# A scheduler's price for changing the matmul shape: 0.1 between three kinds becomes 0.175 between two

## The chip, the core and the metric

The kernel runs on one core of one Trainium2 chip. A core has five engines, each with an instruction queue of its own that it works through in order: TensorE (PE in the profile; its weight loads are listed as PEld), VectorE (DVE), ScalarE (ACT), GpSimd (POOL) and SyncE (SP), which here issues the DMAs. Engines wait for each other through semaphores. The metric is the device time of one execution in microseconds (us), the median of several runs.

## The reference

A retention layer (attention with a causal decay instead of a softmax) for 8 batches of 8 heads, 576 positions, 64 wide, and then an MLP with a PReLU on the 4608 x 512 result. All is fp32.

```python
scores = scale * np.matmul(q, k.transpose(0, 1, 3, 2))
gamma = 1.0 - 2.0 ** (-5.0 - np.arange(H, dtype=np.float32))
rel = pos[:, None] - pos[None, :]
Dmat = np.where(rel >= 0, gamma[:, None, None] ** rel[None, :, :], 0.0)
x = np.matmul(scores * Dmat[None], v)        # then (B,H,S,D) -> (B*S, H*D)
h = x @ w_in                                 # 512 -> 2048
g = np.maximum(h, 0.0) + alpha * np.minimum(h, 0.0)
return g @ w_out                             # 2048 -> 512
```

## The kernel before

**Retention** is computed in chunks of 64 positions, nine to a head. Inside a chunk there are scores (k times q, masked) and their product with v; what earlier chunks contribute is carried in a state, the decayed sum of k times v, one 64 x 64 matrix a chunk. The matrices are 64 wide, so these matmuls use a quarter or a half of the 128 x 128 array, several side by side. Two forms occur. The first batches' heads are done in "parts" of four chunks with all eight heads together: `part_transposes` (full array), `part_scores` (L503), `part_states` (L526), `part_values` (L574, L599, L615) and `last_part` for the ninth chunk. Their loads are scaled on POOL by `part_scale` (L455). The rest is done for pairs of heads in `joint`: 24 joints, each with the scores and states of one pair (L913, L920, L923, named "x" and "su") and the values of the pair before (L861, "v0" and "v1"). Between a joint's states and its values lie DVE and ACT work and SP's copies of the masked operand (at<-qT) and of the sums (vn<-su).

**The MLP** is cut into blocks of 256 tokens (18) and units of 256 hidden columns (8). Eight early cells are computed in plain fp32 (`unit_plain` L1091, `second_plain` L1122). All others use pieces: each operand is split into a high and a low part in a faster fp32 format (fp32r), and three products are summed: `unit_roll` (L1188) and `unit_two` (L1222) for x @ w_in, `second` (L1340) and `second_last` (L1284) for g @ w_out. ACT, DVE and POOL make the pieces: weights are first brought to a suitable form in `convert` (ACT L730 and L732, DVE L740, L742 and L751, POOL L754) and split in `split_w`; hidden values are split in `split_g`. Before the first real work PE multiplies an identity matrix with itself (`fill`, L1405), 18 times in all.

**The order** is not written by hand. The kernel's code first records operations with `do(engine, cost, function, reads, writes, ..., kind=, size=)`: the engine, a cost in us estimated by the author, and what is read and written, from which the dependencies follow. `dues` walks this graph backwards and gives each operation a due time. `plan` then walks forwards and makes the order: on each engine it takes, of the operations that could start within a small slack of the earliest (0.2 us on PE), the one with the least due time. `earliest` says when an operation could start. Among its terms are the time at which the engine is free, the operands, the PSUM banks, the DMA bytes under way, the fetching of PE's instructions in chunks of 256 (`size` counts them), and a price for a change of `kind` on the same engine:

```python
return t + SWITCH.get(op.eng, 0.0) * (kinds[op.eng] != op.kind)
```

Only PE has such a price. Its operations are of three kinds: "small" for all 64-wide matmuls of the retention, "pieces" for the matmuls of the MLP's pieces, and "PE", the default, for transposes, fills and plain fp32 matmuls. `do` sets the kind to the engine's name where none is given.

After a first plan, `plan` is run again with due times from the plan so far (12 times), and then 243 times with due times disturbed at random in one stretch of 40 us; the plan with the shortest estimated total is kept. Last, the functions are called in that order, so it becomes the order of the instructions on each engine, and of SP's DMAs.

Of the kernel before, what the change touches and what calls it, by code (L numbers as in the profile page):

```python
# [21 lines left out]
def kernel(  # L22
# [322 lines left out]
    EARLY, JOINTS = 1, {(s, i): 1 for s in range(14) for i in range(2) if (s, i) not in ((0, 0), (8, 1), (10, 1), (13, 0), (13, 1))}  # L345
    PUMP0, PUMP = ((1, 2), (0, 1), (0, 1), (0, 1)), ((1, 2), (1, 2), (0, 1), (0, 1))
    GROUPS = (("v0",), ("v1",), ("x", "su"))
    SLACK, SWITCH = {"PE": 0.2}, {"PE": 0.1}
    BEGIN = {"PE": 1.9, "ACT": 0.5, "DVE": 5.5, "POOL": 5.4, "SP": 0.5}


# [348 lines left out]
    pieces = []  # L700
# [5 lines left out]
    w_at = {}  # L706
# [460 lines left out]
    def unit_roll(some, u, f, fine):  # L1167
        sides = [vis["kb"] % 2 for vis in some]
        wide = len(some) == 2
        cols = slice(0, DM) if wide else slice(sides[0] * TB, (sides[0] + 1) * TB)  # L1170
        p0, p1 = (Gen(x) for x in (psa if f else psh))

        def xp(l, cc):
            r = [row_x(side, l) + cc for side in sides]
            t = lx_all("x")[:, r[0]:r[1] + 1:r[1] - r[0]] if wide else lx_all("x")[:, r[0]]
            return piece(t)

        def out_of(p):
            t = p.get()[:, cols]
            return t.rearrange("p (s t) -> p s t", s=2) if wide else t  # L1180
        for some_l in (((p0, 0),), ((p0, 1),), ((p1, 2),)) if fine else (
                ((p0, 0), (p0, 1), (p1, 2)),):
            def mm(some_l=some_l):
                for p, l in some_l:
                    for cc in range(NCC):
                        w = w_piece(u, cc // 2, l)
                        c0 = (cc % 2 * 2 + f) * P
                        nc.tensor.matmul(out_of(p), w[:, c0:c0 + P], xp(l, cc),  # L1188
                                         start=(l != 1 and cc == 0), stop=(l > 0 and cc == NCC - 1))
            ls = [l for _, l in some_l]  # L1190
            do("PE", (0.911 if wide else 0.483) * len(ls), mm,
               [(vis["x"], l, n) for vis in some for l in ls for n in range(2)] +
               [w_at[u, i][l] for i in range(2) for l in ls],
               [(p, 0) for p in (p0, p1) if any(p is q for q, _ in some_l)], size=8 * len(ls), kind="pieces")
        return p0, p1, out_of

    def acts_roll(ps, gens, g, u, f):
# [14 lines left out]
    def unit_two(va, vb, u, outs, f):  # L1212
        at_x = va["x"][0]
        p0, p1 = (Gen(x) for x in (psa if f else psh))

        def mm():
            for p, l in ((p0, 0), (p1, 2), (p0, 1)):
                for cc in range(NCC):
                    w = w_piece(u, cc // 2, l)
                    c0 = (cc % 2 * 2 + f) * P  # L1220
                    g, o = at_x[l, cc]
                    nc.tensor.matmul(p.get(), w[:, c0:c0 + P], piece(words_of(g)[:, o:o + DM]),  # L1222
                                     start=(l != 1 and cc == 0), stop=(l > 0 and cc == NCC - 1))
        do("PE", 2.73, mm, x_keys(va, 0) + x_keys(vb, 1) +
           [w_at[u, i][l] for i in range(2) for l in range(3)], [(p0, 0), (p1, 0)], size=24, kind="pieces")
        fc = 2 * u + f
        for cols, gens, g in outs:
            def both(x):
                o = g(f)
                return x.rearrange("p (s t) -> p s t", s=2) if len(o.shape) == 3 else x  # L1230
            keys = [(ga, f) for ga in gens]
            do("ACT", 0.59, lambda: nc.scalar.copy(g(f), both(p1.get())), [(p1, 0)], keys)
            do("DVE", 0.69, lambda: nc.vector.scalar_tensor_tensor(
                out=g(f), in0=both(p0.get()), scalar=ONE, in1=g(f), op0=ALU.mult,
                op1=ALU.subtract), [(p0, 0)], keys)
            do("ACT", 0.62, lambda: nc.scalar.activation(
                both(p1.get()), g(f), ACTF.Relu, scale=-1.0), keys, [(p1, 0)])
            do("DVE", 0.75, lambda: nc.vector.scalar_tensor_tensor(
                out=g(f), in0=both(p1.get()), scalar=malpha[:, fc:fc + 1], in1=g(f),
                op0=ALU.mult, op1=ALU.add), [(p1, 0), (cst, "a")], keys)  # L1240
# [30 lines left out]
    acc = []  # L1271
# [3 lines left out]
    def second_last(c0, c1):  # L1275
        vis = c1["vis"]

        def mm(cell, m, to, terms, first, last, cols=slice(0, DM)):
            g, u = cell["g"], cell["u"]

            def f(a=list(to)):
                for f in range(2):
                    for b, l in terms:
                        nc.tensor.matmul(a[b].get()[:, cols],  # L1284
                                         piece(g.get()[:, l, f, m * P:(m + 1) * P]),
                                         w_piece(u, 2 + f, l)[:, cols],
                                         start=(first and f == 0 and l != 1),
                                         stop=(last and f == 1 and l > 0))
            wide = cols.stop - cols.start == DM
            op = do("PE", (0.459 if wide else 0.241) * len(terms), f, [(g, l) for _, l in terms] +  # L1290
               [w_at[u, i][l] for i in (2, 3) for _, l in terms],
               [(to[b], 0) for b in sorted({b for b, _ in terms})], size=4 * len(terms),
               kind="pieces")
            op.deps += [o for o in chain if o not in op.deps]
            chain[:] = [op]
        chain = []
        sums, rests = ((0, 0), (0, 1)), ((1, 2),)
        mm(c0, 1, acc[2:4], rests, False, True)
        mm(c0, 1, acc[2:4], sums, False, True)
        was, t = vis["o"], lambda: vis["o"].get()[:, 1]  # L1300
        do("DVE", 0.69, lambda p=acc[3]: nc.vector.tensor_tensor(
            out=t(), in0=p.get(), in1=t(), op=ALU.subtract), [(acc[3], 0)], [(was, 1)])
        do("DVE", 0.69, lambda p=acc[2]: nc.vector.scalar_tensor_tensor(
            out=t(), in0=p.get(), scalar=ONE, in1=t(), op0=ALU.mult, op1=ALU.subtract),
            [(acc[2], 0)], [(was, 1)])
        mm(c0, 0, acc[0:2], sums + rests, False, False)
        d = Gen(psa[0])
        mm(c1, 1, (None, d), rests, True, True)
        do("DVE", 0.69, lambda: nc.vector.tensor_tensor(
            out=t(), in0=d.get(), in1=t(), op=ALU.subtract), [(d, 0)], [(was, 1)])  # L1310
        mm(c1, 0, acc[0:2], rests, False, True)
        mm(c1, 0, acc[0:2], sums, False, True)
        evacuate(vis, 0)
        ends = [Gen(psh[0]), Gen(psh[1])]
        o, t0 = Gen(os_[1]), vis["kb"] * TB + P
        for n, p in enumerate(ends):
            cols = slice(n * TB, (n + 1) * TB)
            mm(c1, 1, (p,), sums, True, True, cols)
            do("DVE", 0.42, lambda p=p, cols=cols: nc.vector.scalar_tensor_tensor(  # L1319
                out=o.get()[:, cols], in0=p.get()[:, cols], scalar=ONE, in1=t()[:, cols],  # L1320
                op0=ALU.mult, op1=ALU.subtract), [(p, 0), (was, 1)], [(o, n)])
            dma(lambda cols=cols: out[t0:t0 + P, cols], lambda cols=cols: o.get()[:, cols],
                P * TB * 4, [(o, n)], [(okm[vis["kb"]], "e", n)], eng=("ACT", "SP")[n])

    def second(cell):
# [7 lines left out]
        for m in range(2):  # L1333

            terms = ((0, 0), (0, 1)), ((1, 2),)
            for some in reversed(terms) if cell["last"] else (sum(terms, ()),):
                def mm(m=m, a=list(acc), some=some):
                    for f in range(2):
                        for b, l in some:
                            nc.tensor.matmul(a[2 * m + b].get(),  # L1340
                                             piece(g.get()[:, l, f, m * P:(m + 1) * P]),
                                             w_piece(u, 2 + f, l),
                                             start=(cell["first"] and f == 0 and l != 1),
                                             stop=(cell["last"] and f == 1 and l > 0))
                do("PE", 0.459 * len(some), mm, [(g, l) for _, l in some] +
                   [w_at[u, i][l] for i in (2, 3) for _, l in some],
                   [(acc[2 * m + b], 0) for b in sorted({b for b, _ in some})], size=4 * len(some), kind="pieces")
            if cell["last"]:
                evacuate(vis, m)

# [397 lines left out]
```

## Time and profile before

| what | value |
|---|---|
| runs | 919.32 us median of 3 (918.11 to 922.28) |
| the profiled execution | span 917.4 us, 19097 instructions |
| its granted TensorE clock | 1.000 |
| HBM | 74.19 MB read, 32.51 MB written |
| L1340 (`second`), matmuls into pso from w and g | 1392, 338.8 us, mean 391 ns |
| L1188 (`unit_roll`), into psh and psa | 720, 172.0 us, mean 379 and 376 ns |
| L861, values of the joints | 864 records, 32.3 us, mean 226 ns |
| L920 and L923, scores and states of the joints | 1536 records, 55.2 us, mean 218 and 223 ns |

The span is the time from the first to the last instruction of one execution; the time of a run holds a little more. Matmuls overlap: one lasts 391 ns from its start to its end, but the next starts much sooner, so that a busy time is the union of such stretches and a mean is no price. An fp32 matmul (L861 and the other lines of the retention, L1091, L1122) leaves two records for each matmul of the program, one of pieces leaves one. Behind each entry of the timeline stands, in brackets, how long its engine was idle before it and what ended that. PEld is the loading of the stationary operand, which runs beside the matmuls.

### The profile page before, as it was taken

Reading aid. Unit: us, or ns where it says so; the run is one execution under the profiler, and the core shown is the slowest. Engines: PE = TensorE matmul, PEld = TensorE weight load, DVE = VectorE, ACT = ScalarE, POOL = GpSimd, SP = SyncE. Lnnn points to the kernel's source line nnn. Section 1 sums busy time; section 2 is a strip of 40 time slices with the busy share of each in tenths; the row PEclk is TensorE's granted clock in tenths of the full one; section 3 lists DMA queues with packets and bytes.
Section 4 is the critical chain, followed back from the end, with each engine's and each line's share of the span. In section 5 each row is a group of like instructions: output and inputs, shape, how many; then the busy total and the mean of one; then the engine's idle time right before and its main releaser. Section 6 shows DMA issues by size and latency. Waiting matters only on the chain. (4 is left out here: it accounts for less than half of the span.)

```text
span 917.4 us, 19097 instructions
## 1 busy us (share of the span) xinstructions
PE 906.9 (99%) x7289; PEld 737.8 (80%) x7289; DVE 548.0 (60%) x1003; ACT 503.9 (55%) x1010; POOL 520.2 (57%) x461
## 2 busy tenths in 40 slices
PE   7999999999999999999999999999999999999998
PEld 6767688887888888888888888888888888888886
DVE  5786766667677667676757776344444534344343
ACT  4575455646565656565746555537463636364441
POOL 4776746456466665674542244665656656574624
PEclk9999999999999999999999999999999999999999
DMA  9995688977988879895243332212121322211112
GB/s 216 251 235 86 164 189 186 198 178 155 221 192 194 209 166 201 193 189 181 93 138 130 102 125 65 86 57 81 58 89 56 99 73 86 74 64 47 47 46 69
DMA packets 235947, 121.32 MB, mean 132 GB/s; under 512 B 203456, under 2 KB 203728, under 8 KB 235856
## 3 DMA queue, kind: packets, MB, share of 16 engines
q1 hardware_dynamic: 235712, 119.98, 52.1%
q8 instruction: 57, 0.93, 0.4%
q14 instruction: 34, 0.28, 0.1%
q10 hardware_dynamic: 144, 0.13, 0.0%
HBM read 74.19 MB, written 32.51 MB: 116 GB/s over the span
## 5 line engine op out<-in xcount | busy, mean ns | idle before, releaser
L1340 PE MATMUL pso<-w,g 128*128 128x512 f32 x1392 | 338.8, 391 | 0.0
L1340 PEld LDWEIGHTS pso<-w,g 128*128 128x128 f32 x1392 | 258.9, 188 | 55.2 <-POOL g L1267 1.2
L1264 POOL TENSOR_TENSOR g<-ga_all,g 128x512 fp32r<-128x512 f32 x76 | 97.9, 1291 | 130.4 <-ACT g L1260 105.0
L1267 POOL TENSOR_TENSOR g<-g 128x512 fp32r<-128x512 f32 x114 | 147.4, 1294 | 23.7 <-DVE su L1066 5.7
L1188 PE MATMUL psh<-lx_x,w 128*128 128x512 f32 (+1 forms) x360 | 86.6, 379 | 0.0
L1188 PE MATMUL psa<-lx_x,w 128*128 128x512 f32 (+1 forms) x360 | 85.4, 376 | 0.0
L1188 PEld LDWEIGHTS psa<-lx_x,w 128*128 128x128 f32 x360 | 65.1, 188 | 13.1 <-issue 0.4
L1188 PEld LDWEIGHTS psh<-lx_x,w 128*128 128x128 f32 x360 | 64.2, 188 | 12.9
L1260 ACT ACTIVATE g<-ga_all 128x512 fp32r<-128x512 f32 x76 | 47.6, 631 | 43.0 <-PE pso L1340 21.0
L1256 POOL TENSOR_TENSOR g<-g 128x512 fp32r<-128x512 f32 x22 | 28.5, 1296 | 64.0 <-DVE g L1253 38.3
L1264 POOL TENSOR_TENSOR g<-vn,g 128x512 fp32r<-128x512 f32 x25 | 32.4, 1297 | 37.5 <-ACT g L1260 34.9
L1340 PE MATMUL pso<-lx_x,g 128*128 128x512 f32 x216 | 53.5, 390 | 0.1
L1163 POOL TENSOR_TENSOR lx_x<-lx_x 128x512 fp32r<-128x512 f32 x28 | 35.9, 1294 | 26.0 <-DVE lx_x L1160 26.0
L941 DVE SCALAR_TENSOR_TENSOR at<-psa,pf,mask 64x512 f32<-64x512 f32 x48 | 36.0, 749 | 21.1 <-PE psh L861 10.2
L1340 PEld LDWEIGHTS pso<-lx_x,g 128*128 128x128 f32 x216 | 40.4, 188 | 9.0 <-DVE o L1363 0.7
L1262 ACT ACTIVATE g<-ga_all 128x512 fp32r<-128x512 f32 x76 | 47.2, 621 | 0.0
L1358 DVE TENSOR_TENSOR op<-pso,op 128x512 f32<-128x512 f32 x35 | 24.0, 686 | 31.3 <-PE pso L1340 31.2
L1202 ACT COPY ga_all<-psh 128x512 f32<-128x512 f32 (+1 forms) x30 | 16.7, 558 | 39.1 <-PE psh L1188 37.4
L861 PEld LDWEIGHTS psh<-at,vn 128*64 128x64 f32 x864 | 27.9, 137 | 8.7 <-issue 3.6
L1222 PE MATMUL psh<-w,w 128*128 128x512 f32 x144 | 34.6, 389 | 0.0
L1222 PE MATMUL psa<-w,w 128*128 128x512 f32 x144 | 34.6, 389 | 0.0
L754 POOL TENSOR_TENSOR wa<-wa,op 128x512 int32<-128x512 int32 x16 | 21.0, 1311 | 23.1 <-DVE wa L751 19.1
(329 smaller groups left out, 1883.3 us busy)
## 6 DMA issues: line engine op xcount, KB each, us to landing
xk<-x SPq DMA_DIRECT2D x18, 512.0 KB, 3.7
ok<-o SPq DMA_DIRECT2D x36, 256.0 KB, 2.9
op<-ok SPq DMA_DIRECT2D x18, 512.0 KB, 3.9
out_dram<-o SPq DMA_DIRECT2D x35, 256.0 KB, 2.3
x<-xk SPq DMA_DIRECT2D x16, 512.0 KB, 5.6
qx<-in_q_dram SPq DMA_DIRECT2D x96, 72.0 KB, 3.4
kx<-in_k_dram SPq DMA_DIRECT2D x96, 72.0 KB, 3.3
kn<-in_k_dram SPq DMA_DIRECT2D x48, 144.0 KB, 3.4
```

The source lines that it names most:

```text
L861: nc.tensor.matmul(pv[i].get()[half(h2), (j - js[0]) * C:(j - js[0] + 1) * C], vns[n % 2][:, h2, j], mt.get()[:, h2, j], start=True, stop= ...
L941: nc.vector.scalar_tensor_tensor(out=mt.get()[half(1 - h2), h2, j], in0=fro[x], scalar=pf[x, 1, h:h + 1], in1=mask[x, None, :].to_broadcas ...
L1163: do("POOL", 1.29, lambda h=h, l=l, d=d: nc.gpsimd.tensor_tensor(out=piece(d()), in0=h(), in1=l(), op=ALU.subtract), [(g, 0, n), (g, 1, n) ...
L1188: nc.tensor.matmul(out_of(p), w[:, c0:c0 + P], xp(l, cc), start=(l != 1 and cc == 0), stop=(l > 0 and cc == NCC - 1))
L1222: nc.tensor.matmul(p.get(), w[:, c0:c0 + P], piece(words_of(g)[:, o:o + DM]), start=(l != 1 and cc == 0), stop=(l > 0 and cc == NCC - 1))
L1256: do("POOL", 1.29, lambda: nc.gpsimd.tensor_tensor(out=piece(to.get()[:, 2]), in0=to.get()[:, 0], in1=to.get()[:, 1], op=ALU.subtract), [( ...
L1260: do("ACT", 0.64, lambda: nc.scalar.mul(piece(to.get()[:, 2]), whole(), BELOW), both, [(to, 2)])
L1262: do("ACT", 0.64, lambda: nc.scalar.mul(piece(to.get()[:, 0]), whole(), BELOW * 2.0 ** -12), both, [(to, 0)])
L1264: do("POOL", 1.29, lambda: nc.gpsimd.tensor_tensor(out=piece(to.get()[:, 1]), in0=whole(), in1=to.get()[:, 2], op=ALU.subtract), both + [( ...
L1267: do("POOL", 1.29, lambda: nc.gpsimd.tensor_tensor(out=piece(to.get()[:, 2]), in0=to.get()[:, 0], in1=to.get()[:, 1], op=ALU.subtract), [( ...
L1340: nc.tensor.matmul(a[2 * m + b].get(), piece(g.get()[:, l, f, m * P:(m + 1) * P]), w_piece(u, 2 + f, l), start=(cell["first"] and f == 0 a ...
L1358: do("DVE", 0.69, lambda: nc.vector.tensor_tensor(out=t(), in0=p1.get(), in1=t(), op=ALU.subtract), [(p1, 0)], [tk])
```

## The change

The price for a change of kind on PE goes from 0.1 to 0.175 us. The four places that recorded the matmuls of the pieces with the kind "pieces" (in `unit_roll`, `unit_two`, `second_last` and `second`) now record them as "PE", the kind of the transposes, the fills and the plain fp32 matmuls. So the scheduler counts 0.175 between "small" and everything else, and nothing between fp32 and pieces. No operation, cost or dependency is changed.

```diff
-    SLACK, SWITCH = {"PE": 0.2}, {"PE": 0.1}
+    SLACK, SWITCH = {"PE": 0.2}, {"PE": 0.175}
...
-               [(p, 0) for p in (p0, p1) if any(p is q for q, _ in some_l)], size=8 * len(ls), kind="pieces")
+               [(p, 0) for p in (p0, p1) if any(p is q for q, _ in some_l)], size=8 * len(ls), kind="PE")
...
-           [w_at[u, i][l] for i in range(2) for l in range(3)], [(p0, 0), (p1, 0)], size=24, kind="pieces")
+           [w_at[u, i][l] for i in range(2) for l in range(3)], [(p0, 0), (p1, 0)], size=24, kind="PE")
...
-               kind="pieces")
+               kind="PE")
...
-                   [(acc[2 * m + b], 0) for b in sorted({b for b, _ in some})], size=4 * len(some), kind="pieces")
+                   [(acc[2 * m + b], 0) for b in sorted({b for b, _ in some})], size=4 * len(some), kind="PE")
```

## The prediction

> **What bounds the kernel now.** I read the page's first part, then the busy time by stretch, then the timeline at one change of shape, then the timeline of the start.
>
> ```profile
> PE 906.9 (99%) x7289; PEld 737.8 (80%) x7289; DVE 548.0 (60%) x1003; ACT 503.9 (55%) x1010; POOL 520.2 (57%) x461
> ```
>
> TensorE is busy for 906.9 of 917.4 us, and nothing else is over 60%. The stretches show where the other 10.5 us are (after the stretch: its length, then busy time of PE, PEld, DVE, ACT and POOL with instructions, then granted clock, DMA share, GB/s):
>
> ```profile
> 0.00:12.00 12.00, 9.14 (x159) 7.93 (x160) 6.97 (x43) 3.63 (x5) 6.26 (x19) 1.00 0.96 186
> 12.00:24.00 12.00, 9.92 (x281) 8.58 (x274) 7.33 (x15) 7.47 (x13) 5.95 (x6) 1.00 0.96 251
> 24.00:36.00 12.00, 10.69 (x221) 7.39 (x220) 11.34 (x20) 7.26 (x15) 7.71 (x8) 1.00 1.00 233
> 36.00:48.00 12.00, 12.00 (x142) 8.85 (x143) 7.01 (x13) 6.10 (x11) 8.63 (x9) 1.00 1.05 266
> 102.00:222.00 120.00, 119.85 (x1328) 97.16 (x1328) 80.91 (x156) 66.86 (x145) 65.07 (x54) 1.00 0.84 183
> 222.00:420.00 198.00, 198.00 (x2072) 162.37 (x2070) 139.17 (x265) 121.82 (x248) 124.31 (x99) 1.00 0.86 195
> 420.00:906.00 486.00, 485.87 (x2272) 401.96 (x2267) 246.77 (x410) 258.34 (x512) 262.37 (x236) 1.00 0.26 82
> ```
>
> PE idles 2.86 + 2.08 + 1.31 us before 36 us (1.69 of it before its first instruction), 0.15 in 102 to 222, none in 222 to 420, and 3.9 in the last 11 us, the final evacuation. So the end is set by the sum of PE's work, plus the waits of the start. A schedule can save in two places: the cost of changing shape on PE, and those waits.
>
> **What a change of shape costs.** One joint of the attention, start, length, instructions:
>
> ```profile
> 299.62 3.79 PE L1340 MATMUL pso<-w,g 128*128 128x512 f32 x16
> ...
> 303.34 0.27 PE L913 MATMUL psh<-qT,kT 64*64 64x64 f32 x2
> ...
> 304.38 0.22 PE L920 MATMUL psa<-qT,kT 64*64 64x64 f32 x2
> ...
> 304.54 1.27 PE L861 MATMUL psh<-at,vn 128*64 128x64 f32 x36
> 305.73 1.20 PE L1188 MATMUL psh<-lx_x,w 128*128 128x512 f32 x4
> ```
>
> Sixteen piece matmuls take 3.79 with 0.39 for one (L1340's mean of 391 ns), so they start (3.79 - 0.39) / 15 = 0.227 apart. The sixteenth starts at 303.03, its successor would at 303.25, and L913 starts at 303.34: going in costs 0.09. L861's 36 records end at 305.81; one lasts 0.226, so the last starts at 305.58, the 36 start (305.58 - 304.54) / 35 = 0.03 apart, and the next piece matmul comes 0.15 after it: coming out costs 0.15 - 0.03 = 0.12. Between L920 (64x64) and L861 (128x64), both "small" to the scheduler, it is again 304.54 - 304.39 = 0.15, so 0.12. Round trip: 0.21. The scheduler before counts 0.1 each way, so 0.2: its price is already right, and 0.175 each way is too high. That between fp32 and pieces nothing is due fits the two such changes of this trace, which show no added time (0.12 from a narrow piece matmul to L1122, the narrow ones' own step).
>
> **The change, part by part.** No instruction is added or removed: each matmul line has the same number of matmuls in both built programs. What moves is the order on all five engines, almost everywhere. In PE's order of the two programs I counted the runs of small matmuls between wide ones: 54 before, 45 after. In the joints, where values (L861) and scores with states (L913, L920, L923) had stood apart or been cut in two, they mostly stand as one run of 52; changes between those two shapes inside a run go from 22 to 27. So
>
> - 9 fewer ways in, at 0.09: -0.8 us
> - 9 fewer ways out, at 0.12: -1.1 us
> - 5 more changes inside small runs, at 0.12: +0.6 us
> - 2 more changes between fp32 and pieces: 0
>
> together -1.3 us. It is all on the path, since PE has no idle time that could hide it. The Trainium skill, "TensorEngine Tiling (Array Packing)", Key Properties, says that changing the tiling mode drains TensorE while changing the tile does not. By it the 128x64 to 64x64 step is a mode change as much as the others; the row above agrees (0.15), and this speaks against the change: five of the nine runs saved are only half saved. A sum that took all small shapes as one mode would have been 9 x 0.21 = 1.9 us.
>
> **The start is reordered too,** and this is the unknown. Lines of before:
>
> ```profile
> 4.17 1.12 PE L479 MATMUL psa<-ident,w 128*128 128x128 f32 x4
> 6.99 2.15 POOL L455 TENSOR_TENSOR w<-w,tp 128x512 f32<-128x512 f32 x2 [3.88 <-DMA w<-in_q_dram]
> 8.11 0.66 PE L479 MATMUL pso<-ident,w 128*128 128x128 f32 x4 [0.69 <-POOL w L455]
> 15.86 0.34 PE L574 MATMUL pso<-g,w 64*64 64x64 f32 x7 [1.32 <-issue]
> 18.50 0.69 DVE L740 TENSOR_SCALAR psa<-ga_all 128x512 f32<-128x512 f32 x1 [4.14 <-ACT ga_all L730]
> 23.11 1.99 PE L1091 MATMUL psh<-x,lx_w 128*128 128x256 f32 x8 [0.43 <-POOL lx_w L754]
> 30.49 0.27 PE L599 MATMUL psa<-w,w 64*64 64x64 f32 x2 [1.03 <-ACT spy L588]
> ```
>
> Two moves count. First, SP fetches one half of part 0's v ahead of q, and POOL scales it ahead of q: q is ready one L455 later (2.15 / 2 = 1.07 us), and its transposes, scores, masks and values wait behind it on PE, ACT and DVE. Second, part 1's transposes (16 matmuls: 0.49 + 1.02 + 0.49 = 2.0 us of PE) no longer fill part 0's gaps; instead SP fetches the first four 256 KB loads of w_in ahead of part 1's k and most of its q, so DVE need not idle its 4.14 us until 18.50 and the conversions (L740 to L751, about 2.2 us of DVE each, DVE being 11.34 of 12 busy in 24 to 36) start some 3.5 us sooner. The first plain MLP unit (L1091) then can start near 20 rather than 23.11. By about 23.5 both orders have done the same amount: 18.3 + 1.1 for the late q, less 1.5 of transposes, plus the 2.5 of fills gives a start of L1091 at some 20.0 to 20.4 and 8 of its matmuls (3.46 us) done by then; before has by then the transposes (2.0), the scores (0.95) and 0.4 of L1091. After that the last q half of part 1 waits for POOL, which has the fourth conversion ahead of it (DVE's four conversions from 15.0 on end near 24.3, POOL's 1.29 and 1.04 near 26.6), while PE gets there at 25.0: a wait of 1.6. Against it stand the three later waits of before that sooner conversions can close: 0.43 at 23.11, 1.03 at 30.49, 0.5 around it, 1.9 together. Net -0.3, which I take. Bounds: all 4.56 us of idle time before 36 (6.25 less the 1.69) closed, -4.6; none closed, the 1.6 paid and the stall of 1.32 at 15.86, which the trace puts down to issue, met once more because 144 small matmuls now stand in one row: +2.9, and 1.1 for q: +4.0.
>
> **The sum.** The profiled execution has 917.4 of span; the median of the runs is 919.32, 1.9 more, and I predict on the median: 919.3 - 1.3 - 0.3 = 917.7. 0.5% of it, about what a measurement of this kernel can tell from no change, is 4.6 us, so the sum is within it. The likeliest case's own range is 914.8 to 922.0: the two bounds of the start, cut in at each end since both need everything to fall one way.
>
> **Rivals.**
>
> *The start gives back most of its waits.* For it: DVE's 4.14 us of idleness is the longest wait of the early stretch and the new order removes it. Against: DMA is at 0.96 to 1.05 through 48 us, so less can be brought forward than PE could use. All 4.56 closed: 919.3 - 1.3 - 4.6 = 913.4; over 0.5% faster needs 3.3 of the 4.56. Chance 0.17.
>
> *A late transfer in the joints: slower.* A joint's values (L861) need the sums that SP copies (vn<-su). SP issues in order, and its order is new; where four loads of the next pair (qx, 2.67 us to issue in the timeline at 303.26) get ahead of that copy, L861 waits, and PE, in order too, has everything behind it. Price: up to 2.67 us for each joint hit, of 24. Against: in 102 to 420 before, PE idles 0.15 us. From three such waits on it decides: 917.7 + 3 x 2.67 = 925.7. Chance 0.21.
>
> *The cold clock.* Four transposes take 1.12 us at 4.17 and 0.66 at 8.11, so PE runs at half speed at first. The new order has PE idle between its last early fill (about 7.2) and the late q (about 9.1). If that put the clock back, the next 4 us of PE work would double where it binds: +2 us, 919.7. The Trainium skill, "TensorE: Matmul & The Clock Gate", has the clock fall only after an idle window of some 3.4 us, which 1.9 is not; by that rule nothing is lost. Chance 0.05.
>
> That the change does not act is excluded by the counted orders.
>
> **Chances and range.** The forecast has 0.57, rivals 0.17, 0.21, 0.05. Faster by over 0.5%: 0.17; slower: 0.21; within: 0.62. The range 913.8 to 924.0 takes in the forecast and the clock, most of the first rival and the second up to two waits, leaving out some 0.2.
>
> **What would show it.** Right: about nine fewer changes of shape on PE, each still 0.09 in and 0.12 out; PE at 100% from 48 us on; L1091 first near 20; an early PE idle sum of 3 to 6 us. Wrong: idle PE before L861 put down to vn<-su; a PE idle sum in the first 48 us off by over 3 us either way; ways out that cost more in the longer runs.

## The result, and the profile after

The changed kernel takes 924.38 us (median of 4 runs, 924.27 to 924.59) beside 919.57 for the kernel before on the same chip (4 runs, 918.11 to 922.28): ratio 1.0051, 95% interval 1.0035 to 1.0068. That is slower by 0.5%, 0.4 us above the top of the predicted range, where 0.2% faster was forecast. The profiled execution has a span of 922.7, 5.3 more than before's 917.4.

The first part of the page of the changed kernel:

```profile
PE 910.0 (99%) x7289; PEld 738.7 (80%) x7289; DVE 548.4 (59%) x1003; ACT 504.1 (55%) x1010; POOL 519.8 (56%) x461
```

PE is busy for 3.1 us more with the same 7289 records, and idle for the other 2.2 us. The busy time by stretch of the changed kernel (length, then PE, PEld, DVE, ACT, POOL with instructions, granted clock, DMA share, GB/s), for the stretches shown of before and the one that was left out there:

```profile
0.00:12.00 12.00, 7.64 (x56) 6.19 (x60) 7.31 (x41) 3.58 (x6) 6.21 (x19) 0.90 0.97 219
12.00:24.00 12.00, 11.02 (x307) 9.95 (x300) 9.65 (x16) 7.30 (x13) 4.88 (x5) 0.82 1.00 257
24.00:36.00 12.00, 11.28 (x168) 7.89 (x167) 9.89 (x18) 6.74 (x12) 8.76 (x9) 1.00 1.07 217
36.00:48.00 12.00, 11.73 (x197) 8.57 (x195) 6.18 (x13) 5.28 (x10) 8.17 (x9) 1.00 0.96 235
48.00:102.00 54.00, 53.63 (x824) 37.17 (x821) 40.75 (x73) 32.79 (x66) 38.15 (x33) 1.00 0.64 154
102.00:222.00 120.00, 118.25 (x1357) 95.20 (x1356) 80.99 (x159) 65.15 (x142) 65.84 (x54) 1.00 0.85 186
222.00:420.00 198.00, 197.78 (x2066) 162.32 (x2065) 139.82 (x266) 122.69 (x251) 123.06 (x99) 1.00 0.84 189
420.00:906.00 486.00, 486.00 (x2285) 401.66 (x2284) 246.00 (x410) 259.30 (x513) 260.59 (x235) 1.00 0.27 83
```

The idle time of the first 48 us is what it was (4.36 + 0.98 + 0.72 + 0.27 = 6.33, before 6.25), though it lies elsewhere. New is 1.75 in 102 to 222, where there had been 0.15. The timeline of the changed kernel shows it at the end of the plain fp32 MLP, where the first matmul of the pieces (L1188) starts:

```profile
98.47 0.47 DVE L955 SCALAR_TENSOR_TENSOR psa<-su,gch,psa 128x256 f32<-128x256 f32 x1
...
105.67 0.92 PE L861 MATMUL psh<-at,vn 128*64 128x64 f32 x24 [0.35 <-DVE ga_all L1102]
106.52 1.98 PE L1122 MATMUL pso<-g,ga_all 128*128 128x512 f32 x4
...
108.82 0.58 DVE L941 SCALAR_TENSOR_TENSOR at<-psh,pf,mask 64x64 f32<-64x64 f32 x2
109.55 1.66 PE L1188 MATMUL psh<-lx_x,w 128*128 128x256 f32 x12 [1.04 <-DVE at L941]
```

The same place in the timeline of the kernel before:

```profile
94.30 0.47 DVE L955 SCALAR_TENSOR_TENSOR psa<-su,gch,psa 128x256 f32<-128x256 f32 x1
...
103.88 0.58 DVE L941 SCALAR_TENSOR_TENSOR at<-psh,pf,mask 64x64 f32<-64x64 f32 x2
...
105.00 1.04 PE L1188 MATMUL psa<-lx_x,w 128*128 128x256 f32 x4
```

L1188 had started at 105.00 with no wait; now it starts at 109.55 after 1.04 of idleness, when DVE's L941 has read the PSUM buffer psh that L1188 writes. In the 12.9 us ahead of it DVE is idle for only 1.1 (0.9 of 12.2 in the same work of before): it is late as a whole. Its first L955, the sum of the first joint's states, comes at 98.47 in place of 94.30. So of the 5.28 us by which PE's last matmul ends later (913.68 before, 918.96 after), 4.55 are there before the MLP of the pieces begins. The 24 joints add 0.09 (first matmul of pieces to last 64-wide one: 330.31 before, 330.40 after), and what follows them 0.64.

Most of the 4.55 is not idle time. A record of L1122 lasts about 0.6 us though the next starts 0.429 after it, so a wait of up to 0.17 leaves no gap. I therefore made a tally from the starts alone: at each moment, the clock time less the sum of the usual steps of all matmuls started so far (the usual step of a line and shape is its median in the trace of before; a mean for the 64-wide ones). Against before, the changed kernel has lost 0.4 us by 36 us, 5.0 by 140, 5.2 by 900. The loss is made between 36 and 140 us, 3.8 of it up to 112. (With another mean for the 64-wide matmuls the figures of this tally move by up to about 0.5.)

### The profile page after: what moved, and what is told of

It is laid out like the page before. It is cut to its first block, busy times and chain, and to the rows that moved or that the text cites. A ratio compares the mean times of both kernels' runs of the same rounds, so it can differ in the third digit from the quotient of the medians.

```text
span 922.7 us, 19112 instructions
## 1 busy us (share of the span) xinstructions
PE 910.0 (99%) x7289; PEld 738.7 (80%) x7289; DVE 548.4 (59%) x1003; ACT 504.1 (55%) x1010; POOL 519.8 (56%) x461
## 5 line engine op out<-in xcount | busy, mean ns | idle before, releaser
L1188 PE MATMUL psh<-lx_x,w 128*128 128x512 f32 (+1 forms) x360 | 87.9, 381 | 1.4 <-DVE at L941 1.0
L1188 PE MATMUL psa<-lx_x,w 128*128 128x512 f32 (+1 forms) x360 | 84.4, 375 | 0.0
L1188 PEld LDWEIGHTS psh<-lx_x,w 128*128 128x128 f32 x360 | 64.1, 188 | 16.1 <-POOL lx_x L1163 1.8
L1188 PEld LDWEIGHTS psa<-lx_x,w 128*128 128x128 f32 x360 | 64.8, 188 | 12.9 <-ACT ga_all L1202 0.3
L941 DVE SCALAR_TENSOR_TENSOR at<-psa,pf,mask 64x512 f32<-64x512 f32 x48 | 36.0, 750 | 26.1 <-PE psa L920 16.8
L861 PEld LDWEIGHTS psh<-at,vn 128*64 128x64 f32 x864 | 28.0, 137 | 8.4 <-issue 3.9
```

The lines of the kernel that those rows point to most:

```text
L861: nc.tensor.matmul(pv[i].get()[half(h2), (j - js[0]) * C:(j - js[0] + 1) * C], vns[n % 2][:, h2, j], mt.get()[:, h2, j], start=True, stop= ...
L941: nc.vector.scalar_tensor_tensor(out=mt.get()[half(1 - h2), h2, j], in0=fro[x], scalar=pf[x, 1, h:h + 1], in1=mask[x, None, :].to_broadcas ...
L1188: nc.tensor.matmul(out_of(p), w[:, c0:c0 + P], xp(l, cc), start=(l != 1 and cc == 0), stop=(l > 0 and cc == NCC - 1))
```

## The experiments

Each kernel was timed in five rounds beside the kernel before. In the expectations, "start" is everything ahead of the first matmul of the pieces for the first two kernels and the first 36 to 48 us elsewhere; "plain stretch" is what follows up to some 110 us, where 64-wide matmuls alternate with plain fp32 ones; "joints" is 110 to 440 us.

**Which part of the order costs the time?** Four kernels have the order written out instead of planned. The first has before's order up to the first matmul of the pieces and the changed one behind it, the second the reverse, the third before's order for some 36 us only.

```diff
-    for op in best[1]:
+    for op in (ops[n] for n in ORDER):
```

> The order is written out: up to the first piece matmul it is that of the kernel before, from there on that of the changed one. Theory 'start': 4.55 of the 5.28 us by which the changed kernel's PE ends later are there at its first piece matmul (109.55 against 105.00 us), so this kernel takes 919.6 + 0.1 (joints) + 0.6 (behind the joints) = 920.3, +-1.0. Rival 'joints': the longer runs of small matmuls cost, and the start only shifts when things are done: 923 or more.

> The reverse: the changed kernel's order up to the first piece matmul, that of the kernel before from there on. Theory 'start': 924.4 - 0.7 = 923.7, +-1.0. Rival 'joints': 921 or less.

> The order of the kernel before for the first 36 us or so, that of the changed kernel from there on. If the first 36 us (late q, clock at half from 9.5 to 16.4 us) make the loss, about 920.5. If it is made by the changed order between 36 and 110 us (the wait of 1.4 us before the first L1188 and smaller ones), 923 to 924.

Measured: 923.04 (ratio 1.0035, 1.0022 to 1.0047), 924.84 (1.0053, 1.0041 to 1.0066) and 927.15 (1.0080, 1.0066 to 1.0094). The second supports the plain stretch: with the changed order there and before's joints, it is as slow as the whole change (0.1 above the range expected). The first misses its 920.3 and meets the rival's "923 or more", which puts the loss into the joints. Its timeline shows waits at the seam that neither kernel has:

```profile
116.32 0.92 PE L861 MATMUL psh<-at,vn 128*64 128x64 f32 x24 [0.47 <-DVE ga_all L1203]
117.98 0.33 PE L913 MATMUL psh<-qT,kT 64*64 64x64 f32 x4 [0.74 <-DVE ga_all L1208]
```

So 1.2 us of idleness at least belong to the joining, of 3.4 us lost. The trace speaks against the joints all the same: counted from the starts, the first kernel has lost 1.0 us by 112 us, loses 2.7 right behind the seam, from 112 to 140 (the changed kernel 1.1), and nothing more from 140 to 900. The third waits 2.1 us at 40.5 us, near its seam, which spoils its time; but L1188 still waits 1.04 for L941 in it, with before's first 36 us ahead. Orders of five engines can't be cut and joined cleanly; I went on by changing what the scheduler counts.

**The clock.** In the stretches above the clock is 0.90 and 0.82 where before had 1.00: at half speed for 12 x 0.10 / 0.5 = 2.4 and 12 x 0.18 / 0.5 = 4.3 us. The fourth kernel has the changed order and eleven more fills on PE ahead of the late q.

```diff
+        for _ in range({14: 8, 16: 3}.get(op.n, 0)):
+            nc.tensor.matmul(unread.get()[:, 0:P], ident, ident, start=True, stop=True)
```

> The changed kernel's order with 11 more fills on PE, 8 ahead of the first and 3 ahead of the second transposes of q, where PE idles 1.85 and 0.75 us, and nothing else moved. Theory 'clock': the idle time put the clock to half; filled, it stays at full speed from 6 us on, and the about 2 us that the small matmuls lose between 9.5 and 16.4 us come back: 922.4 or less. Rival: the clock stays up, but the later waits of the start (0.45 and 0.6 us at 26 to 28 us for POOL and ACT, 1.4 at 108) take the gain: 924.0 +-0.4. If the clock falls all the same, idle time is not what lowers it: 924.4 and half clock in the same stretch.

Measured: 925.48 (1.0065, 1.0051 to 1.0079). In its busy time by stretch the clock stays up at first and falls later, for 3.4 us:

```profile
0.00:12.00 12.00, 10.13 (x114) 9.13 (x118) 7.19 (x41) 4.05 (x6) 6.23 (x19) 1.00 0.99 218
12.00:24.00 12.00, 8.85 (x267) 7.97 (x257) 10.25 (x17) 6.97 (x12) 5.48 (x5) 0.86 0.99 258
```

Half the slow-clock time is gone and no time is won; the kernel is above both ranges expected (922.4 or less, 924.0 +-0.4), as L574 stands 2.2 us at 16.7 where the changed kernel has 0.8. By the tally, with the fills counted as work, it is level with before at 36 us and loses 4.4 from 36 to 140 all the same, and one of its executions has a mean granted clock of 1.000 and took 925.09. So the clock isn't the cause of that loss.

**Price or kinds, and luck.** The change has two parts: 0.1 becomes 0.175, and pieces lose their kind. Since the scheduler searches at random, the same two kernels were also planned with the search begun elsewhere.

```diff
f1: SWITCH 0.175 in the kernel before (three kinds)
-    SLACK, SWITCH = {"PE": 0.2}, {"PE": 0.1}
+    SLACK, SWITCH = {"PE": 0.2}, {"PE": 0.175}
f2: SWITCH 0.1 in the changed kernel (two kinds)
-    SLACK, SWITCH = {"PE": 0.2}, {"PE": 0.175}
+    SLACK, SWITCH = {"PE": 0.2}, {"PE": 0.1}
f3 (before), f4 (changed):
-    rng = np.random.RandomState(1)
+    rng = np.random.RandomState(2)
```

> The kernel before with the price at 0.175 and its three kinds kept, planned anew. Theory 'price': the higher price alone makes the scheduler hold small matmuls back and buy waits elsewhere, so this is as slow as the changed kernel: 923.5 to 925.5. Rival 'luck': the search for a plan ends elsewhere after any edit, by several us: anything from 917 to 927, and not with the change's order. Rival 'kinds': the merging of the kinds does it, and this is 919 to 921.

> The changed kernel with the price at 0.1, so only the kinds are merged. Theory 'price': 919 to 921, as there are next to no changes between fp32 and pieces to be priced. Rival 'kinds': 923.5 or more. Rival 'luck': anything from 917 to 927.

> The kernel before with another seed of the search's random disturbances. Theory 'price': within 1.5 us of 919.6. Rival 'luck': as likely 2 to 5 us off as not.

> The changed kernel with the other seed. Theory 'price': within 1.5 us of 924.4. Rival 'luck': as likely at 919 to 922 as at 924.

Measured: 924.70 (1.0061, 1.0049 to 1.0073) for the price alone; 921.12 (1.0016, 1.0003 to 1.0029) for the kinds alone; with the other search 919.60 (1.0017, 0.9999 to 1.0035) for before and 925.77 (1.0068, 1.0056 to 1.0081) for the changed kernel. It is mainly the price (the kinds add 0.2%, at the edge of what can be told), and with two searches for each kernel it doesn't look like luck: begun elsewhere, the search leaves both where they were within 1.5 us, and the distance between them stays.

**Where the price acts, and through what.** Its place was divided first (g1: 0.175 only where pieces are on one side; g2: only where they are not). Then its two uses were divided. `earliest` returns one number, which both chooses the operation and becomes its planned begin. In g3 the slack within which the choice is free grows by as much as the price. In g4 the choice sees 0.175 and the planned time counts 0.1.

```diff
g1 (before; g2 has 0.1 and 0.175 the other way round):
-            return t + SWITCH.get(op.eng, 0.0) * (kinds[op.eng] != op.kind)
+            return t + (kinds[op.eng] != op.kind and op.eng == "PE") * (0.175 if "pieces" in (kinds[op.eng], op.kind) else 0.1)
g3 (changed kernel):
-    SLACK, SWITCH = {"PE": 0.2}, {"PE": 0.175}
+    SLACK, SWITCH = {"PE": 0.275}, {"PE": 0.175}
g4 (changed kernel):
-            begin[op.n] = t
+            t -= 0.075 * (op.eng == "PE" and kinds[op.eng] != op.kind); begin[op.n] = t
```

> The kernel before with its three kinds; the price is 0.175 where pieces are on one side of the change and 0.1 otherwise, so the stretch ahead of the first piece matmul (small between plain fp32 matmuls) is priced as before and the joints as in the changed kernel. Theory 'plain stretch' (the higher price does its harm where small matmuls alternate with plain fp32 ones, up to 110 us): first piece matmul by 106 us, 918.5 to 921. Rival 'everywhere': 922 to 924.

> The reverse: 0.175 between small and plain fp32 matmuls, 0.1 where pieces are on one side. Theory 'plain stretch': first piece matmul at 109 us or later, 923 to 926. Rival 'everywhere': 921 to 923.

> The changed kernel with PE's slack at 0.275 instead of 0.2: an operation of the other kind may again be ready up to 0.1 us after the earliest and still be chosen by its due time (0.025 in the changed kernel). Theory 'choice' (with 0.175 the more urgent operation of the other kind loses to whatever is ready in the kind that runs): 919 to 921.5, and 46 or more changes of shape ahead of the first piece matmul against 40. Rival 'clock of the plan' (each change makes the planned PE 0.075 us later, and what the other engines do is timed to that): no better than 923.5.

> The changed kernel with the price of 0.175 in the choice of the next operation, and 0.1 of it in the planned time. Theory 'choice': 923.5 or more, with some 40 changes of shape ahead of the first piece matmul. Rival 'clock of the plan': 919 to 921.5.

Measured: g1 921.70 (1.0020, 1.0010 to 1.0029), between the two theories' ranges, with the first matmul of pieces at 106.1; g2 926.20 (1.0065, 1.0046 to 1.0083); g3 927.76 (1.0092, 1.0075 to 1.0108), so that more freedom of choice cures nothing; g4 919.82 (1.0004, 0.9994 to 1.0014), as fast as before. g2 is 0.2 above the range expected; g3 has 44 changes ahead of the first matmul of pieces. The busy time of g2 in two stretches:

```profile
36.00:102.00 66.00, 62.47 (x1001) 43.68 (x998) 43.40 (x76) 36.45 (x72) 43.00 (x39) 1.00 0.72 164
...
102.00:140.00 38.00, 35.92 (x443) 27.86 (x442) 27.29 (x59) 18.38 (x45) 22.22 (x18) 1.00 0.75 163
```

and of g4:

```profile
36.00:102.00 66.00, 65.02 (x956) 45.51 (x954) 51.36 (x94) 38.32 (x74) 46.70 (x41) 1.00 0.77 173
102.00:140.00 38.00, 38.00 (x461) 30.47 (x462) 24.81 (x49) 21.38 (x48) 20.15 (x17) 1.00 0.84 194
```

In 36 to 102 us DVE, the third of the five pairs, gets 43.40 us of work done in g2 and 51.36 in g4; after 102 us PE idles 2.1 us in g2 and never in g4. The higher price as a preference is harmless; counted as time it costs what the change costs. The reading, which no run shows directly: it makes the plan run PE later, and with it the work that PE waits for.

**Why does a price nearer to the truth plan worse?** What remained was where the plan's PE time is wrong. The costs beside the traces give a candidate. An operation of plain fp32 matmuls (L1096 and L1126, 16 of each) is counted 1.86 us, while the traces show 8 steps of 0.216 or 4 of 0.429: 1.73 or 1.72. Operations of pieces are counted at 0.911 for four steps of 0.227, which is 0.908. So in the plain stretch, and only there, the cost of a change of shape may already be in the costs. Four more kernels take that apart: the changed kernel with 1.73 (h1, and h4 with the other search), before with 1.73 (h2), and before with 1.99 (h3), which adds planned time without touching the price.

```diff
h1, h2, h4 (h3: 1.99), here and in the same place of unit_plain:
-            do("PE", 1.86, mm, [(ga, 0), (ga, 1), plain[4 * u + 2], plain[4 * u + 3]],
+            do("PE", 1.73, mm, [(ga, 0), (ga, 1), plain[4 * u + 2], plain[4 * u + 3]],
```

> The changed kernel, with the cost that the scheduler counts for an operation of plain fp32 matmuls (L1096 and L1126, 32 of them) set from 1.86 to 1.73 us, which is what the traces show for them (4 x 0.429 and 8 x 0.216). Price 0.175 as changed. Theory 'PE's planned time is too late in the plain stretch, whatever makes it so': 32 x 0.13 = 4.2 us come off the planned time, about what 40 changes at 0.175 in place of 48 at 0.1 put on with what was there; first piece matmul back to 104 to 106.5, time 918.5 to 921.5. Rival 'it is the price itself, in its place at the changes of shape, and not the sum of the planned time': first piece 109 to 112, time 923.5 to 926.

> The kernel before with the same two costs at 1.73. If a planned time that is too late is what hurts, the 1.4 us or so that the plan of before may be late are gone too: not slower than before, 917 to 920.5, first piece 103 to 105.5. If a plan that is too early hurts as much as one that is too late, slower: 921.5 to 925.

> The kernel before, price 0.1 and three kinds, with the two costs at 1.99 in place of 1.86: 4.2 us more planned time of PE in the plain stretch and nothing else. Theory 'planned time too late': as slow as the changed kernel without any part of its change, 923 to 927, first piece 109 to 112. Rival 'the price in its place': 918.5 to 921.5, first piece 104 to 106.5.

> As the changed kernel with 1.73, with the scheduler's random search begun from 2 in place of 1 (the changed kernel from 2 took 925.8, before from 2 919.6). Theory 'planned time too late': 918.5 to 921.5, first piece 103 to 106.5. Rival 'the price in its place': 924 to 927, first piece 109 to 112.

Measured: h1 922.33 (1.0034, 1.0023 to 1.0045), h2 925.47 (1.0063, 1.0046 to 1.0081), h3 928.94 (1.0117, 1.0093 to 1.0141), h4 923.71 (1.0050, 1.0034 to 1.0066). h3 is as expected and more: with no part of the change it is slower than the changed kernel. h1 and h4 are 2.1 us better than their counterparts with 1.86, not the 4 expected, and lie between the theory and its rival: h4's first matmul of pieces starts at 109.3, where the rival has it. h2 comes out slower, its second alternative (921.5 to 925 expected). The tally says where. For all planned kernels, in us of the profiled execution, beside before's: the span; the time lost up to 36 us, from 36 to 140, and from 140 to 900; and in the last column by how much the plan counts more for the plain stretch than the chip needs. That is 32 operations at their counted cost and the changes of shape ahead of the first matmul of pieces at the planned price, less 128 x 0.216 + 64 x 0.429 = 55.1 and 0.18 a change (the price that the traces show, worked out in the next section).

| kernel | plan's price, cost | changes | span | to 36 | 36 to 140 | 140 to 900 | counted too much |
|---|---|---|---|---|---|---|---|
| before | 0.1, 1.86 | 48 | 0 | 0 | 0 | 0 | 0.6 |
| changed | 0.175, 1.86 | 40 | +5.3 | +0.4 | +4.6 | +0.2 | 4.2 |
| f1 | 0.175, 1.86 | 38 | +6.8 | -2.6 | +8.9 | +0.3 | 4.2 |
| f2 | 0.1, 1.86 | 52 | +2.2 | +0.8 | +0.5 | +0.6 | 0.3 |
| f3 | 0.1, 1.86 | 50 | -1.2 | -1.6 | +1.2 | -0.8 | 0.4 |
| f4 | 0.175, 1.86 | 40 | +6.9 | -1.7 | +7.0 | +1.5 | 4.2 |
| g1 | 0.1 there, 1.86 | 50 | +4.1 | +1.2 | +1.4 | +1.4 | 0.4 |
| g2 | 0.175 there, 1.86 | 40 | +7.6 | -1.5 | +7.7 | +1.0 | 4.2 |
| g3 | 0.175, 1.86 | 44 | +8.2 | +2.2 | +5.1 | +0.8 | 4.2 |
| g4 | 0.1, 1.86 | 48 | +0.3 | -0.8 | +0.7 | +0.3 | 0.6 |
| h1 | 0.175, 1.73 | 46 | +2.7 | +1.6 | +1.2 | -0.6 | 0.0 |
| h2 | 0.1, 1.73 | 42 | +7.3 | +6.0 | +0.5 | +0.6 | -3.1 |
| h3 | 0.1, 1.99 | 42 | +9.1 | +2.0 | +5.3 | +1.7 | 5.2 |
| h4 | 0.175, 1.73 | 46 | +4.5 | +3.5 | +1.5 | -0.6 | 0.0 |

The column from 36 to 140 falls into two groups with nothing between them. Every plan that counts 4 us or more too much for PE loses 4.6 to 8.9 us there, and every plan that counts 0.6 or less too much loses 0.5 to 1.5. The price is in both groups (0.175 with 1.73 is in the good one, 0.1 with 1.99 in the bad one), so it isn't the price in its place but the sum that it makes. Two cautions. h2 and h4 reach 36 us already 6.0 and 3.5 us late, so the other engines had that much more time: their small loss behind it may be one already paid, and without them only h1 carries the price of 0.175 in the good group. And f1 and f4 have a granted clock of 0.97 in 36 to 102 us, each for one stretch of 3.4 us at half speed, worth at most 1.7 of their 8.9 and 7.0; in the other four of the bad group it is 1.00.

The busy time of DVE in 36 to 102 us divides the kernels in the same way (50.0 to 51.5 us in the good group, 41.9 to 46.9 in the bad one). Before, and below it the changed kernel:

```profile
36.00:102.00 66.00, 65.88 (x958) 46.46 (x956) 50.97 (x93) 38.56 (x74) 47.21 (x42) 1.00 0.76 176
36.00:102.00 66.00, 65.36 (x1015) 45.75 (x1014) 46.93 (x85) 38.07 (x75) 46.32 (x41) 1.00 0.70 168
```

h1:

```profile
36.00:102.00 66.00, 66.00 (x959) 46.40 (x963) 50.17 (x90) 39.93 (x76) 46.30 (x40) 1.00 0.75 175
```

and h3:

```profile
36.00:102.00 66.00, 64.36 (x1010) 44.71 (x1009) 45.89 (x84) 35.65 (x71) 44.46 (x40) 1.00 0.68 161
```

What 1.73 wins there h1, h2 and h4 lose in the first 36 us, 1.6 to 6.0 us. Among h2's waits on PE (engine and line, what it waited for, total, times, longest) is one for nothing that the profile shows, of a length that no other kernel has:

```profile
PE psh L1405 <- issue: 4.1, 1, 4.1
```

The clock adds to it: from 12 to 36 us h2's granted clock is 0.86 and then 0.72, and h4's is between 0.83 and 0.88 from the start to 36 us, in each some 10 us at half speed; h1's is 1.00. That a plan that counts too little does this is likely and isn't shown: g3 and h3 lose 2 us there too. No kernel tried is clearly faster than before.

## Why the prediction was wrong

**What bounds the kernel: right.** PE is at 99% before and after.

**The failed step is the term for the new order: "Net -0.3, which I take. Bounds: ... -4.6 ... +4.0", with "PE at 100% from 48 us on".** It followed the new order up to 36 us and took for granted that the stretch behind it would stay full, because it was full before. For its own 36 us it was not bad: the tally gives +0.4 for a forecast of -0.3. The late q came. The timeline of the changed kernel:

```profile
8.89 0.66 PE L479 MATMUL pso<-ident,w 128*128 128x128 f32 x4 [1.85 <-POOL w L455]
10.30 1.11 PE L479 MATMUL pso<-ident,w 128*128 128x128 f32 x4 [0.75 <-POOL w L455]
...
21.59 1.96 PE L1091 MATMUL psh<-x,lx_w 128*128 128x256 f32 x8
```

PE waits 1.85 + 0.75 for q where before lost 0.69 + 0.4, so 1.5 more for a predicted 1.1, and L1091 starts at 21.59, between the predicted 20 and the 23.11 of before. The predicted wait of 1.6 for the last half of part 1's q came as 0.29 + 0.43, at 26.80 and 27.89. The loss came behind: +4.6 us between 36 and 140, a stretch for which the sum had no term. DVE's and POOL's order there was new like PE's, and no line of before could say that PE would find its operands ready. A bound for the unknown should have had a loss in that stretch as well.

**The price of a change of shape: the mechanism right, two terms missing.** In 0.09 and out 0.12 hold after the change. But the second matmul behind a way out is late as well, which the prediction's own quoted rows show: x4 of L1188 take 1.20 right behind L861, where 3 x 0.227 + 0.39 = 1.07 are due. In the timeline of a joint of the changed kernel:

```profile
281.52 1.27 PE L861 MATMUL psh<-at,vn 128*64 128x64 f32 x36
282.72 2.12 PE L1340 MATMUL pso<-w,g 128*128 128x512 f32 x8
```

Eight take 2.12, where 7 x 0.227 + 0.39 = 1.98 are due: the same 0.13 or so. Between the starts themselves I find 0.335 in place of 0.227, thus 0.11 more. In fp32 the steps of L1122 have a median of 0.429 and a second group at 0.533, L1091's 0.216 and 0.320, thus 0.10. The way in has a second part too: the second pair of L861 starts 0.100 after the first where the later pairs are 0.052 apart, and for L913 it is 0.073 and 0.025, thus 0.05 more. The round trip is 0.09 + 0.05 + 0.12 + 0.11 = 0.37, some 0.18 each way, and "0.175 each way is too high" was wrong: it is the nearer price. As a change of shape inside a 64-wide run has that second part as well (0.12 + 0.05), the saving should have been 9 x 0.37 - 5 x 0.17 = 2.5 us and not 1.3.

**The saving: counted rightly, not found.** PE's changes between wide and 64-wide shapes go from 48 to 40 ahead of the first matmul of pieces and from 60 to 50 behind it, nine runs as predicted. For the joints, five round trips fewer and four inner changes more (the fifth lies ahead of them, at 104.75) make 5 x 0.37 - 4 x 0.17 = 1.2 us less by these prices; the joints took 0.09 longer. Over the kernels of the table their changes behind that point go from 50 to 62 with no visible relation to the last lost-time column. Where it went in the joints is not settled; no single wait holds it.

**The rivals.** *The start gives back its waits* (0.17): no, but its premise was right in part, since L1091 starts 1.5 us sooner. *A late transfer in the joints* (0.21) had the sign and nearly the size, 925.7 against 924.4, by the wrong mechanism. The waits of the changed kernel on PE:

```profile
PE pso L479 <- POOL w L455: 2.6, 2, 1.8
...
PE psh L1188 <- DVE at L941: 1.0, 1, 1.0
...
PE psh L861 <- DMA vn<-su: 0.2, 1, 0.2
```

vn<-su holds L861 up once, for 0.2 us, as before. *The cold clock* (0.05): it did fall, for longer than the 4 us assumed, and cost little or nothing at the end. The tally has lost 1.5 us at 12 us and 0.4 at 36, and e4 wins nothing by keeping the clock up at first.

**What the price did instead.** It has two uses. In the choice, 0.175 for 0.1 changes nothing in the time (g4). In the planned begin of every operation on PE it makes the plan's PE run later than the chip's where shapes alternate with plain fp32 matmuls, on top of costs that hold half of it already (32 x 1.86 is 4.4 over the 55.1 of the traces): with 0.1 the sum was 0.6 us too much, with 0.175 it is 4.2. The other engines' orders would then be made for a PE that is late, and the operation that the early PE needs would stand behind others. L941, 4.9 us later than before while L1188 waits for its buffer, is what it looks like. That planned time is the cause of the loss between 36 and 140 us is shown by g4, which takes the price out of the time alone, and by h3, which adds time without the price; h1 supports that it is the sum, though its whole time came back by 2.1 us only. That it works through the other engines' orders, and which operations on DVE, ACT and POOL change places, is argued from such lines and was not tried.

## What to carry to other kernels

A number in a planner's cost model can be a preference and a clock at once; try the two uses apart, and when one price is made truer, look for the costs that had been set with the old one and hold part of it. A better local price is no better plan: compare the planned and the measured time of each stretch, and forecast a reordered stretch by its operands on the other engines, not by PE having been full in the old order. Where records overlap, count lost time from start to start, since idle time showed less than half of it here.

## What the runs showed of the hardware

- The clock fell in the changed kernel at about 9.6 us (12 less the 2.4 us at half speed), with no idle stretch of PE over 1.85 us after its first work; of the 3.4 us ahead of the fall PE was busy for 1.6. Four transposes took 1.11 us at half speed and 0.66 at full. The Trainium skill, "TensorE: Matmul & The Clock Gate", section "What's actually happening", has it fall after an idle window of some 3.4 us; the trace disagrees, as no such stretch was idle throughout.
- Coming back from 64-wide shapes delays not only the next matmul on the whole array (0.12) but also the one after it (0.11). Going to them delays the first one (0.09) and, once more, a group shortly behind it (0.05).
